# A long transform split 64 by 32 instead of 32 by 64, with its short stages as 64-row and 64-column TensorE tiles

## Chip, cores, metric

One core of one Trainium2 chip. The metric is the device time of one execution in microseconds (us), the median of several. A run over 1.5% above the fastest of its kernel is called slow, the others fast; only fast ones are compared here. The median of the kernel before lies between 343.3 and 345.9 us over the rounds, so kernels are compared through their ratio to the kernel before, which ran in the same rounds on the same chip.

## The reference, cut to what matters

```python
def reference(...):
    x = A_u                                             # 1 x 2048 x 640
    g = sigmoid((x * gate_w).sum(-1, keepdims=True))
    a = A(x, ...)     # K[d, l] = Re sum_n C exp(dt A l) dt B ; a = causal convolution of u with K
                      # along l (written with rfft / irfft of length 4096) + u * Dskip
    b = (gelu(x @ w_gate) * (x @ w_up)) @ w_down        # 640 -> 1728 -> 640
    return g * a + (1 - g) * b
```

The kernel does the feed-forward half as ordinary matmuls. The convolution half generates samples of K ("contraction", on TensorE), transforms K and u in two stages A and B, multiplies the spectra ("chain"), and transforms back in two stages (the second one is "finish"). Between two stages the data have to change partitions, and they do that by being written to DRAM (tensors dU, dKA, dY) and read back in another order. The channels are treated in two halves of W = 320.

## The kernel before: what the change and the argument touch

The order of instructions is made by a small list scheduler in the kernel itself (class `Plan`), which knows estimated costs and a table `P` of ranks. It counts every transfer as 0.45 us of SP's time and a fixed time per KB. All working tiles are slices of one large SBUF tile called `arena`.

```python
def contract(h):                                        # samples of K: 640 matmuls of 32 columns for each half
    for b in range(nb):
        for i in range(16):
            for q in range(2):
                for cg in range(4):
                    c = 16 * (b0 + b) + i
                    nc.tensor.matmul(ps[32 * cg:32 * cg + NE, k + b, 32 * i:32 * i + 32],
                                     lhsT=cs2[:, q, c, cg:4 * NE:4], rhs=cs1[:, q, c, cg:128:4],
                                     start=(q == 0), stop=(q == 1))
    ...
    src = kst[32 * cg + e0:32 * cg + e0 + n, :, :]      # stores of the samples to dS, 20 for each half

def stageB(src, key, dst, name, c, R):                  # src is dU[h] or dKA[h], a DRAM tensor [32, 128, W]
    v = src[:].rearrange("i (l k) w -> (i l) k w", l=4)
    dma(640, lambda: nc.sync.dma_start(out=bi[s][:], in_=v[:, 8 * c:8 * c + 8, :]), r=key, w=[f"bi{s}"], rank=R)
    for a in range(4):
        def go(k, a=a):
            for b in range(2):
                nc.tensor.matmul(ps[:, k + b, 0:W], lhsT=TB[:, 0, :], rhs=bi[s][:, 2 * a + b, :], start=True, stop=True)
        ...

def chain(h, R):
    ...
            for b in range(2):
                for m, x in ((1, U[c]), (2, Us[c])):    # Us is U with real and imaginary rows swapped, by two transfers
                    nc.tensor.matmul(ps[:, k + b, 0:W], lhsT=TB[:, m, :], rhs=x[:, 2 * a + b, :], start=(m == 1), stop=(m == 2))
    ...
    dma(640, lambda c=c, t=t: nc.sync.dma_start(
        out=dY[h][:].rearrange("i (l k) w -> (i l) k w", l=4)[:, 8 * c:8 * c + 8, :], in_=t[:]), ...)
```

## Time and profile before

| | before |
|---|---|
| time, median of 3 (all) | 343.45 us (342.25, 343.45, 344.82) |
| busy PE, DVE, ACT | 79%, 69%, 64% of the profiled 344.3 us |
| contraction 1, first to last piece | 101.4 to 117.7 us |
| contraction 2 | 183.1 to 201.9 us |
| last phase, after contraction 2 | 142 us |

First lines of the profile's page of the kernel before. The rows under "busy tenths" cut the span in 40 slices; a 9 means busy for 90% or more; the DMA row is the mean busy share of 16 DMA engines. PE stands for TensorE's matmuls and PEld for its weight loads, DVE for VectorE, ACT for ScalarE, POOL for GpSimd; SP is SyncE, which issues the transfers (SPq is its queue). L678 is line 678 of the kernel; `ps` is PSUM, where the matmuls write.

```profile
span 344.3 us, 6849 instructions
## 1 busy us (share of the span) xinstructions
PE 273.3 (79%) x2785; PEld 155.4 (45%) x2798; DVE 238.2 (69%) x331; ACT 220.5 (64%) x302; POOL 4.0 (1%) x15
...
PE   0289999988994699999995267439699999899953
...
DMA  7972222455543223453256529757999799996495
GB/s 242 343 247 57 77 78 76 134 171 151 155 116 101 66 34 76 131 182 83 76 146 136 105 38 216 167 166 176 307 344 351 243 295 305 256 345 204 165 321 163
```

Three phases are to be seen: a start of some 100 us in which ACT and DVE generate the samples' factors; a middle; and from about the 28th slice a last phase in which the DMA engines are nearly full. Windows of 20 us from that last phase (length; busy us and number of instructions of PE, PEld, DVE, ACT and POOL in turn; granted TensorE clock as a share of full speed; DMA share; GB/s):

```profile
300.00:320.00 20.00, 19.50 (x138) 13.19 (x137) 18.60 (x26) 9.02 (x14) 0.00 (x0) 1.00 0.81 257
280.00:300.00 20.00, 17.34 (x122) 11.60 (x121) 12.44 (x15) 10.03 (x16) 0.00 (x0) 1.00 1.04 290
```

The chain of waits (the work that ended last, followed back) names, in the last phase, transfers of 640 KB between 3 and 14 us long (start, length, what):

```profile
275.14 7.86 DMA arena<-dU
282.99 9.39 DMA arena<-dKA
292.39 14.44 DMA arena<-dY
...
321.94 2.92 DMA dY<-arena
```

The second contraction on PE (start, length, line, count, and in brackets the idle time before). PE is idle for 2 to 5 us between pieces although nothing that the profile shows holds it ("issue"):

```profile
183.08 1.52 PE L678 MATMUL ps<-arena 128*20 128x32 bf16 x161
186.74 1.24 PE L678 MATMUL ps<-arena 128*20 128x32 bf16 x128 [2.14 <-issue]
193.21 1.24 PE L678 MATMUL ps<-arena 128*20 128x32 bf16 x128 [5.23 <-issue]
196.94 1.25 PE L678 MATMUL ps<-arena 128*20 128x32 bf16 x128 [2.48 <-issue]
```

### The profile page before, as it was taken

The page shows a single profiled execution, that of the slowest core. Times are in us where ns is not written, and L with a number is a line of the kernel's source. Part 1 is how long each engine was busy: PE and PEld are TensorE (multiplying, and loading weights), DVE is VectorE, ACT ScalarE, POOL GpSimd, SP SyncE. Part 2 cuts the span into 40 slices and gives each one's busy share as a digit, 9 for nine tenths or more (in the row PEclk, how much of TensorE's full clock was granted, in tenths as well). Part 3 has the DMA queues.
Part 4 walks back from the last instruction along what each step waited for, and adds up shares of the span by engine and source line. Part 5 has one row for each costly group of instructions (what it writes and reads, how often), then busy time and mean ns, then how long its engine had stood idle before and what let it go on. Part 6 is the DMA issues. An engine that isn't in the chain of part 4 may idle for free.

```text
span 344.3 us, 6849 instructions
## 1 busy us (share of the span) xinstructions
PE 273.3 (79%) x2785; PEld 155.4 (45%) x2798; DVE 238.2 (69%) x331; ACT 220.5 (64%) x302; POOL 4.0 (1%) x15
## 2 busy tenths in 40 slices
PE   0289999988994699999995267439699999899953
PEld 0044444433673367544443243214346666566731
DVE  5969887999894258698973044524649865799364
ACT  4999986996894499788995046534547853525200
POOL 3000000000000000000000000000000000000000
PEclk9999999999998589999998569858989999999995
DMA  7972222455543223453256529757999799996495
GB/s 242 343 247 57 77 78 76 134 171 151 155 116 101 66 34 76 131 182 83 76 146 136 105 38 216 167 166 176 307 344 351 243 295 305 256 345 204 165 321 163
DMA packets 57989, 60.66 MB, mean 176 GB/s; under 512 B 9475, under 2 KB 53318, under 8 KB 57926
## 3 DMA queue, kind: packets, MB, share of 16 engines
q1 hardware_dynamic: 57958, 60.23, 61.1%
q8 instruction: 22, 0.36, 0.4%
q14 instruction: 9, 0.07, 0.1%
HBM read 35.80 MB, written 19.17 MB: 160 GB/s over the span
## 4 chain that ended last, share of the span: by engine, by line
PE 49%; DMA 25%; SPq 9%; issue 8%; DVE 4%; ACT 2%; DVEq 0%; ACTq 0%
PE ps L530 16%; PE ps L578 12%; PE ps L550 10%; DMA arena<-dY 8%; PE ps L880 4%; SPq L707 3%; PE ps L678 3%; DMA arena<-dKA 3%; ACT arena L289 2%; DMA arena<-in_params_dram 2%; DMA arena<-in_w_gu_dram 2%; DMA arena<-dU 2%; PE ps L748 2%; DMA arena<-in_u_nat_dram 2%; DMA dKA<-arena 2%
## 5 line engine op out<-in xcount | busy, mean ns | idle before, releaser
L289 ACT CAST arena<-ps 128x640 bf16<-128x640 f32 (+2 forms) x110 | 69.4, 692 | 65.8 <-DVE arena L293 26.1
L530 PE MATMUL ps<-arena 128*128 128x512 bf16 x274 | 65.0, 388 | 16.9 <-DMA arena<-in_w_gu_dram 16.0
L550 PE MATMUL ps<-arena 128*128 128x512 bf16 x253 | 63.1, 397 | 13.8 <-DMA arena<-in_w_gu_dram 10.3
L293 DVE CAST arena<-ps 128x640 bf16<-128x640 f32 (+2 forms) x62 | 48.4, 800 | 36.6 <-PE ps L678 21.7
L578 PE MATMUL ps<-arena 128*128 128x320 bf16 x448 | 65.2, 306 | 0.5 <-ACT arena L289 0.3
L578 PEld LDWEIGHTS <-arena 128*128 128x128 bf16 x448 | 44.6, 100 | 19.6 <-issue 1.3
L530 PEld LDWEIGHTS <-arena 128*128 128x128 bf16 x280 | 27.6, 99 | 50.6 <-DMA arena<-in_w_gu_dram 16.0
L550 PEld LDWEIGHTS <-arena 128*128 128x128 bf16 x260 | 26.2, 101 | 46.9 <-DMA arena<-in_w_gu_dram 11.7
L554 DVE TENSOR_TENSOR arena<-ps,arena 128x1024 bf16<-128x1024 f32 x26 | 31.7, 1219 | 18.6 <-PE ps L550 16.2
L618 ACT ACTIVATE arena<-arena 128x2560 bf16<-128x2560 int16 x18 | 41.6, 2340 | 1.6 <-DVE arena L614 1.5
L534 ACT ACTIVATE arena<-ps 128x1024 bf16<-128x1024 f32 (+1 forms) x28 | 27.1, 1024 | 7.6 <-PE ps L530 7.4
L678 PE MATMUL ps<-arena 128*20 128x32 bf16 x1280 | 12.7, 198 | 18.6 <-issue 18.6
L851 PE MATMUL ps<-arena 128*128 128x320 bf16 x128 | 22.6, 310 | 5.6 <-DMA arena<-dU 3.0
L639 DVE TENSOR_TENSOR arena<-arena 128x2560 bf16<-128x2560 bf16 x16 | 23.0, 1484 | 3.8 <-ACT arena L618 3.8
L628 ACT ACTIVATE arena<-arena 128x320 bf16<-128x320 f32 x64 | 23.2, 454 | 0.9 <-DVE arena L481 0.9
L678 PEld LDWEIGHTS <-arena 128*20 128x20 bf16 x1280 | 11.3, 99 | 20.3 <-issue 20.3
L295 DVE TENSOR_SCALAR arena<-ps,omg 128x640 bf16<-128x640 f32 x9 | 7.9, 882 | 18.0 <-PE ps L578 17.9
L851 PEld LDWEIGHTS <-arena 128*128 128x128 bf16 x128 | 12.5, 101 | 14.7 <-DMA arena<-dU 3.8
L880 PE MATMUL ps<-arena 128*128 128x320 bf16 x128 | 18.7, 299 | 0.0
L904 DVE SCALAR_TENSOR_TENSOR arena<-ps,g_f,arena 128x320 bf16<-128x320 f32 x32 | 15.4, 544 | 2.7 <-PE ps L898 2.7
L666 DVE TENSOR_TENSOR arena<-arena 128x2560 bf16<-128x2560 bf16 x10 | 14.9, 1486 | 3.2 <-ACT arena L618 3.1
L612 DVE SCALAR_TENSOR_TENSOR arena<-arena 128x320 int32<-128x320 f32 x40 | 16.9, 483 | 0.0
(89 smaller groups left out, 225.2 us busy)
## 6 DMA issues: line engine op xcount, KB each, us to landing
arena<-in_w_gu_dram SPq DMA_DIRECT2D x52, 160.0 KB
dU<-arena SPq DMA_DIRECT2D x32, 160.0 KB
arena<-dU SPq DMA_DIRECT2D x8, 640.0 KB
arena<-arena SPq DMA_DIRECT2D x16, 320.0 KB
dKA<-arena SPq DMA_DIRECT2D x8, 640.0 KB
arena<-dKA SPq DMA_DIRECT2D x8, 640.0 KB
dY<-arena SPq DMA_DIRECT2D x8, 640.0 KB
arena<-dY SPq DMA_DIRECT2D x8, 640.0 KB
```

The costliest lines, as they stand in the source:

```text
L289: nc.scalar.copy(out=dst, in_=src(b))
L293: nc.vector.tensor_copy(out=dst, in_=src(b))
L530: nc.tensor.matmul(ps[:, k + j, :], lhsT=Wg[w][:, kt, :], rhs=xT[2 * grp + j][:, kt, :], start=(kt == 0), stop=(kt == NKT - 1))
L534: add({"ACT": an(1024)}, lambda s: nc.scalar.activation(out=HTall[0:p, :, f, :], in_=ps[0:p, plan.bank(g):plan.bank(g) + 2, :], func=ACT.G ...
L550: nc.tensor.matmul(ps[:, k + j, :], lhsT=Wu[w][:, kt, :], rhs=xT[2 * grp + j][:, kt, :], start=(kt == 0), stop=(kt == NKT - 1))
L554: add({"DVE": v1(1024)}, lambda s: nc.vector.tensor_tensor(out=HTall[:, :, f, :], in0=ps[:, plan.bank(u):plan.bank(u) + 2, :], in1=HTall[: ...
L578: nc.tensor.matmul(ps[:, k + h, 0:W], lhsT=HTq[q][:, f, 128 * j:128 * j + 128], rhs=Wd[f][:, W * h:W * h + W], start=(f == 0), stop=(f == ...
L618: ac(an(2 * n * W), lambda: nc.scalar.activation(out=t[:], in_=ph.bitcast(I16)[:, :, :, 0:32:2], func=ACT.Sin, scale=SIN_SCALE), r=[f"ph{k ...
L628: nc.scalar.activation(out=cs1[:, 1, :, 4 * s:4 * s + 4], in_=quads(aT[:, ds]), func=ACT.Exp, scale=float(sg * (4 + 8 * i)))
L678: nc.tensor.matmul(ps[32 * cg:32 * cg + NE, k + b, 32 * i:32 * i + 32], lhsT=cs2[:, q, c, cg:4 * NE:4], rhs=cs1[:, q, c, cg:128:4], start= ...
L851: nc.tensor.matmul(ps[:, k + b, 0:W], lhsT=TB[:, 0, :], rhs=bi[s][:, 2 * a + b, :], start=True, stop=True)
L880: nc.tensor.matmul(ps[:, k + b, 0:W], lhsT=TB[:, m, :], rhs=x[:, 2 * a + b, :], start=(m == 1), stop=(m == 2))
```

## The change

The intent: less TensorE work. With a split of 64 by 32 the second, the inverse and the last stage have only 64 rows to sum over, or 64 columns to produce, and four (or two) such matmuls are put on separate quarters (or halves) of the array. The contraction takes four channels ("quads") together in one matmul of 80 columns, and only one quarter of the result is used; its samples then lie on every fourth partition. A third weight buffer, earlier loads and a new table of ranks come with it.

The diff, cut to its core (cuts are marked):

```diff
-    P = dict(sw=5.4, gate=1.91, up=2.5, gelu=8.59, ...)
+    P = dict(sw=40.82, gate=13.77, up=4.13, gelu=8.47, ...)          # 25 values became 38
...
-    Wg = [at(O_W + 1280 * k, [128, NKT, 128], BF16, f"Wg{k}") for k in range(2)]
+    Wg = [at(O_W + 1280 * k, [128, NKT, 128], BF16, f"Wg{k}") for k in range(3)]
...
-    kst = at(O_TAIL + 2560, [128, 32, 80], BF16, "kst")
+    kst = at(O_KST, [128, 80, 80], BF16, "kst")
...
-    dY = [dp.tile([32, 128, W], BF16, name=f"dY{h}") for h in range(2)]
+    dY = [dp.tile([64, 64, W], BF16, name=f"dY{h}") for h in range(2)]
...
     def contract(h):
+            for i in range(n):
+                for q in range(2):
+                    nc.tensor.matmul(ps[:, k + i // g, 80 * (i % g):80 * (i % g) + 80], lhsT=cs1[:, q, k0 + i, :],
+                                     rhs=cs2[:, q, k0 + i, :], start=(q == 0), stop=(q == 1))
...
-                    src = kst[32 * cg + e0:32 * cg + e0 + n, :, :]
+                    src = kv[c:128:4, e0:e0 + n, c, :]               # kv is kst with its columns seen as (e j)
...
     def stageB(src, key, dst, name, c, R):
-        v = src[:].rearrange("i (l k) w -> (i l) k w", l=4)
-        dma(640, lambda: nc.sync.dma_start(out=bi[s][:], in_=v[:, 8 * c:8 * c + 8, :]), r=key, w=[f"bi{s}"], rank=R)
+        v = src[:].rearrange("i (l k s) w -> k (i l) s w", l=2, k=2)
+        dma(640, lambda: nc.sync.dma_start(out=bi[s][:], in_=v[:, :, 8 * c:8 * c + 8, :]), r=key, w=[f"bi{s}"], rank=R)
...
                 for b in range(2):
-                    nc.tensor.matmul(ps[:, k + b, 0:W], lhsT=TB[:, 0, :], rhs=bi[s][:, 2 * a + b, :], start=True, stop=True)
+                    for x in range(2):
+                        nc.tensor.matmul(ps[64 * b:64 * b + 64, k + x, 0:W], lhsT=TB[64 * x:64 * x + 64, 0, :],
+                                         rhs=bi[s][64 * x:64 * x + 64, 2 * a + b, :], start=True, stop=True)
...
-                dma(320, lambda c=c, s=s: nc.sync.dma_start(out=Us[c][64 * s:64 * s + 64], in_=U[c][64 - 64 * s:128 - 64 * s]),
+                dma(320, lambda c=c, s=s: nc.sync.dma_start(out=Us[c][s:128:2], in_=U[c][1 - s:128:2]),
...
-                out=dY[h][:].rearrange("i (l k) w -> (i l) k w", l=4)[:, 8 * c:8 * c + 8, :], in_=t[:]),
+                out=dY[h][:].rearrange("i (k s) w -> k i s w", k=2)[:, :, 8 * c:8 * c + 8, :], in_=t[:]),
...                                                                    (chain and finish: tiles likewise)
```

## The prediction, made before any run of the changed kernel

> **What bounds the kernel now.** No single engine: the page shows PE 79% of 344.3 us, DVE 69%, ACT 64%. The table of 10-us windows shows three phases.
> (1) 0-105 us, to the first kernel contraction (L678): ACT busy 92.7 of the first 110 us, DVE nearly as full; PE starts dense work only at 25 us: the chain of waits runs through parameter and weight loads until then.
> (2) Contractions at 105-118 and 183-202 us, 640 matmuls of 128x32 each. PE is fed too slowly: the chain shows "issue" gaps of 1.2 to 5.2 us between their pieces, and the granted clock falls to 0.50 (windows 110:120, 190:200), so that the next 28 matmuls of L578 take 6.16 us instead of 3.80.
> (3) 202-344 us: transposes through DRAM. DMA share is 0.94 to 1.10 in most windows of 240-310, PE 85-98% busy; the chain alternates DMA (dU, dKA, dY) with PE.
>
> **What the change does.**
> - Contraction: 1280 small matmuls become 320 of 128x80 with K=128 (three quarters of it waste). The logits (80 weight loads with one-column matmuls in 2.1 us) show 26 ns a pair as a floor; 80 columns add at most 33 ns (320 take 136 ns in L880). Estimate 50-60 ns each: 8-10 us a contraction instead of 13 and 19, without the slow clock. Cost: copies out of PSUM grow from 2560 to 6400 columns[...], shared by ACT and DVE.
> - Stages B, chain, finish: L851, L880, L898 are 320 matmuls of about 136 ns, 43 us. [...]
> - DMA: same bytes and run lengths, eight more issues. No gain.
> - Third weight buffer, earlier x and weight loads, new ranks: PE can start near 10 us instead of 25; the 26 us of waits on in_w_gu (L530, L550) mostly go.
> - ACT table loads: 27 against 22 by the order of instructions, 1.28 us each: +6 us.
>
> **On the critical path.** By the new order, ACT has about 83 us of work before it copies contraction 1 (before: about 95), so it lies near 92-98 us, 10 us earlier. From there to contraction 2 ACT has about 83 us (before 67, with 12 idle): unloading moved into this stretch. So contraction 2 starts at 180-188, hardly earlier, but ends at 188-197 instead of 202. Front gain: 8-10 us. Phase 3 holds about 120 us of DMA work (window shares summed from 200 us), so it can't shrink by all of PE's 15-20 us; I take 10-14 us of its 142. Together -18 to -24.
>
> **Prediction: 321 us, 8 in 10 between 307 and 336.** Faster by over 2%: 0.87; within 2%: 0.10; slower: 0.03.
>
> **What would show each step.** L684 under 10 us per contraction, granted clock above 0.5 after it; PE dense from 10 us; contraction 2 over before 197; matmuls of L834 spaced 34-45 ns; PE busy below 250 us; ACT 220-230; the last phase 125-135 us long, DMA share near 1 and a DMA-heavy chain.
>
> **What would make it wrong.** Tiles that don't overlap, or weight loads that block them (phase 3 gains nothing, 330+); copies out of PSUM slower than 1.2 us per 960 columns; contractions bound by ACT rather than PE; or phase 3 bound by PE and latency rather than DMA throughput, in which case more comes (below 307).

The "15-20 us" of PE that the last phase names were the author's estimate of what the tiles save of the 43 us, and the trace of before gave no number for it, so the 10-14 us rest on something not shown (measured later: 10.5 us of PE, e3). The longer copies out of PSUM: added up, their durations in the traces are 14.0 us for both contractions after against 6.7 before, 3.6 us more for each. For 80 columns, a quarter of the 136 ns of L880 is 34; 960 columns took 0.96 us on ACT and 1.16 us on DVE in the changed kernel.

## The result, and the profile after

The changed kernel takes **593.08 us** (592.62 to 593.79, 4 runs) against 343.94 us for the kernel before in the same rounds: a ratio of 1.7256, with a 95% interval from 1.7183 to 1.7329. The result is correct. Ratios here are the mean time of one kernel's fast runs over that of the other's fast runs of the same rounds, so they are not quite the ratio of the medians quoted.

The page of the changed kernel:

```profile
span 591.0 us, 5498 instructions
## 1 busy us (share of the span) xinstructions
PE 287.3 (49%) x2082; PEld 157.2 (27%) x2094; DVE 241.1 (41%) x337; ACT 227.1 (38%) x306; POOL 4.9 (1%) x15
...
PE   3587999259999706346360160244020604246033
...
DMA  8722123114455217324332321121211211342258
GB/s 272 246 56 68 55 77 87 24 38 116 126 157 164 71 55 194 117 77 132 113 112 93 111 96 63 53 92 54 92 53 53 89 52 53 127 128 93 70 135 238
```

The busy times of the engines hardly changed, so the added 249 us are waiting. And the DMA row, which was full in the last phase before, is at 1 and 2 there: the DMA engines are not overloaded, they are *unused*. Two windows of the last phase:

```profile
300.00:320.00 20.00, 5.78 (x38) 2.47 (x36) 7.99 (x10) 8.30 (x10) 0.00 (x0) 0.63 0.13 53
440.00:460.00 20.00, 0.00 (x0) 0.00 (x0) 1.67 (x3) 0.00 (x0) 0.00 (x0) 0.55 0.13 53
```

The last two columns are the key. A share of 0.13 of 16 engines is 2.1 engines, and they move 53 GB/s, that is 26 GB/s for each of two. The slices of the page show the same 52 to 54 GB/s again and again. The chain shows what it is that waits:

```profile
296.55 12.44 DMA arena<-dKA
308.99 31.10 DMA dKA<-arena
...
365.03 30.39 DMA dY<-arena
...
420.25 40.19 DMA arena<-dU
...
484.21 41.79 DMA dY<-arena
```

Transfers of 640 KB that took 3 to 14 us in the chain of before take 12 to 42 us here, queueing included; only the loads from dY stay at 5 to 6. `dKA<-arena` is in this list although its code did not change.

The contraction, on TensorE, did what was hoped. The second one of the changed kernel:

```profile
198.88 3.60 PE L684 MATMUL ps<-arena 128*128 128x80 bf16 x96
230.61 2.46 PE L684 MATMUL ps<-arena 128*128 128x80 bf16 x64
```

160 matmuls in 6.1 us of PE time instead of 640 in pieces spread over 19 us (the gap between the two pieces here is a wait for a transfer), and no "issue" gap. What went are these gaps, 18.6 us over both contractions of the kernel before; PE's busy time on them is the same (12.7 us before, 12.3 after, for both together). The matmuls start 36 ns apart (median).

### The profile page after: what moved, and what is told of

The parts are those of the page before. It is cut to its first block, busy times and chain, and to the rows that moved or that the text cites. A ratio compares the mean times of both kernels' runs of the same rounds, so it can differ in the third digit from the quotient of the medians.

```text
span 591.0 us, 5498 instructions
## 1 busy us (share of the span) xinstructions
PE 287.3 (49%) x2082; PEld 157.2 (27%) x2094; DVE 241.1 (41%) x337; ACT 227.1 (38%) x306; POOL 4.9 (1%) x15
## 4 chain that ended last, share of the span: by engine, by line
DMA 48%; PE 21%; ACT 11%; SPq 10%; DVE 8%; issue 2%; DVEq 0%; ACTq 0%
DMA dY<-arena 17%; DMA arena<-dU 9%; PE ps L580 6%; DMA arena<-dKA 6%; DMA dKA<-arena 5%; PE ps L532 5%; PE ps L552 5%; SPq L845 4%; DMA arena<-dS 4%; ACT arena L291 3%; SPq L829 3%; DMA dS<-arena 2%; ACT arena L630 2%; DMA arena<-dY 2%; DVE arena L556 2%
## 5 line engine op out<-in xcount | busy, mean ns | idle before, releaser
L291 ACT CAST arena<-ps 128x640 bf16<-128x640 f32 (+1 forms) x112 | 73.6, 719 | 238.5 <-PE ps L834 166.4
L295 DVE CAST arena<-ps 128x640 bf16<-128x640 f32 (+1 forms) x62 | 50.5, 841 | 214.0 <-PE ps L834 127.1
L834 PE MATMUL ps<-arena 64*64 64x320 bf16 x256 | 22.2, 422 | 165.6 <-DMA arena<-dKA 81.3
L580 PE MATMUL ps<-arena 128*128 128x320 bf16 x448 | 77.0, 339 | 23.8 <-ACT arena L291 16.3
L532 PE MATMUL ps<-arena 128*128 128x512 bf16 x274 | 68.4, 405 | 19.6 <-DMA arena<-in_u_T_dram 9.1
L552 PE MATMUL ps<-arena 128*128 128x512 bf16 x254 | 61.3, 396 | 2.2 <-DMA arena<-in_w_gu_dram 1.1
L834 PEld LDWEIGHTS <-arena 64*64 64x64 bf16 x256 | 10.0, 138 | 177.7 <-DMA arena<-dKA 83.5
L818 PE MATMUL ps<-arena 128*128 128x320 bf16 x64 | 14.2, 361 | 39.6 <-DMA arena<-dS 24.3
L630 ACT ACTIVATE arena<-arena 128x320 bf16<-128x320 f32 x64 | 23.4, 454 | 6.8 <-DMA dS<-arena 5.9
L885 PE MATMUL ps<-arena 128*64 128x320 bf16 x64 | 8.5, 400 | 31.4 <-DMA arena<-dY 31.3
L658 ACT ACTIVATE arena<-arena 128x320 bf16<-128x320 f32 x40 | 15.0, 456 | 19.8 <-DMA dS<-arena 19.6
L818 PEld LDWEIGHTS <-arena 128*128 128x128 bf16 x64 | 7.1, 113 | 45.9 <-issue 41.9
L661 DVE TENSOR_TENSOR arena<-arena 128x1280 bf16<-128x1280 bf16 x10 | 8.0, 820 | 25.5 <-DMA dS<-arena 17.8
L751 PE MATMUL ps<-arena 128*128 128x320 bf16 x64 | 12.5, 319 | 10.4 <-DMA arena<-in_u_nat_dram 7.2
```

The source lines that it names most:

```text
L291: nc.scalar.copy(out=dst, in_=src(b))
L295: nc.vector.tensor_copy(out=dst, in_=src(b))
L532: nc.tensor.matmul(ps[:, k + j, :], lhsT=Wg[w][:, kt, :], rhs=xT[2 * grp + j][:, kt, :], start=(kt == 0), stop=(kt == NKT - 1))
L552: nc.tensor.matmul(ps[:, k + j, :], lhsT=Wu[w][:, kt, :], rhs=xT[2 * grp + j][:, kt, :], start=(kt == 0), stop=(kt == NKT - 1))
L580: nc.tensor.matmul(ps[:, k + h, 0:W], lhsT=HTq[q][:, f, 128 * j:128 * j + 128], rhs=Wd[f][:, W * h:W * h + W], start=(f == 0), stop=(f == ...
L630: nc.scalar.activation(out=cs1[:, 1, :, 4 * s:4 * s + 4], in_=quads(aT[:, ds]), func=ACT.Exp, scale=float(sg * (4 + 8 * i)))
```

## Experiments

**Theory S** (spread): the 16 loads of stage B and the 8 stores to dY have an access pattern whose outermost dimension has size 2 (`k`), and therefore each runs on 2 of the 16 DMA engines. The trace agrees with two engines (0.13 of 16, at 53 GB/s, in the windows 300:320 and 440:460). The pattern of before, `(i l) k w`, has 128 outermost, and the DMA share there reaches 1.04 (280:300, 290 GB/s). That the outermost dimension is the cause is at this point a conjecture from these two patterns; e1 and e4 test it.
**Rival F**: the change also introduced transfers that step over partitions (`c:128:4`, `s:128:2`), and the trace shows waits that the data do not call for; such false waits string everything up.
**Rival P**: the tiles or the new order themselves are bad.

A transfer of 640 KB at 53 GB/s takes 655,360 B / 53 GB/s = 12.4 us, as the first line of the chain above does; 24 of them are 297 us one after another.

### e1: every such transfer issued as two, of 64 rows each

```diff
-        dma(640, lambda: nc.sync.dma_start(out=bi[s][:], in_=v[:, :, 8 * c:8 * c + 8, :]), r=key, ...)
+        def load():
+            for x in range(2):
+                nc.sync.dma_start(out=bi[s][64 * x:64 * x + 64], in_=v[x, :, 8 * c:8 * c + 8, :])
+        dma(640, load, r=key, ...)
...                                     (the stores to dY likewise)
```

> The changed kernel, but each of the 24 transfers whose access pattern has an outermost dimension of 2 (16 loads of the second stage, 8 stores to dY) is issued as two transfers of 64 rows; nothing else, the engines' order is the same. Theory S (an outermost dimension of 2 puts a transfer on 2 of the 16 DMA engines: 53 GB/s and DMA share 0.13 in the windows 300:320 and 440:460): time falls from 593 to 345-380 us, and no window shows a long stretch at 53 GB/s. Rival F (false waits for transfers with a partition step dominate): stays over 500. Rival P (TensorE tiles or the new order): stays near 590.

Measured: correct, **362.06 us** (360.94 to 363.47), ratio 1.0486 to before (1.0412 to 1.056). One edit of the access patterns takes away 231 of the 249 us. Its page, in the rows that answer to those above:

```profile
DMA  6973230222231025255658687338999998896996
GB/s 218 323 236 94 80 85 19 58 84 80 60 88 29 6 61 154 76 157 140 180 147 205 126 234 198 147 92 188 252 238 306 301 284 263 253 327 191 286 307 176
```

The 9s are back in the last phase, and no slice of it stands at 53 GB/s. A store to dY in its chain:

```profile
286.53 7.37 DMA dY<-arena
```

In its windows 260:280 and 280:300 the DMA share is 1.06 and 1.03, at 270 and 311 GB/s. P is refuted as the main cause: tiles and order are unchanged here.

### e2: without the transfers that step over partitions, spread left as it was

The samples get an SBUF tile of their own instead of a slice of `arena`; the spectrum gets its real and imaginary rows in blocks of 32 partitions, so that the swapping copies move whole blocks.

```diff
+    arenak = mp.tile([128, (K1 - K0) // 2], BF16, name="arenak")     # holds kst and the two trig buffers
...
-    FIELDS = ((0, 1), (2, 15), (1, 1), (1, 31), (0, 1), (0, 63), (6, 1))
+    FIELDS = ((0, 1), (2, 15), (1, 1), (0, 31), (5, 1), (0, 63), (6, 1))
-                    out=Us[c][s:128:2], in_=U[c][1 - s:128:2]),
+                    for b in (32 * s, 64 + 32 * s):
+                        nc.sync.dma_start(out=Us[c][b:b + 32], in_=U[c][b ^ 32:(b ^ 32) + 32])
```

> The changed kernel with its 2-engine transfers left in, but without transfers that step over partitions: the kernel samples lie in a tile of their own, and the spectrum has real rows and imaginary rows in blocks of 32, so that the swapped copy moves whole blocks. Theory S: removes only the waits of ACT for dS between 98 and 131 us, about 25-30 us, and something after 200 us: 540-575 us. Rival F: falls below 420. Rival P: stays near 590.

Measured: correct, **574.52 us** (2 runs), ratio 1.6617. 18.6 us less than the changed kernel: at the upper end of the range for S (I had expected 25 to 30 us from these waits), and far from what F expects. F is a second, small cause.

### e3: both

> Both edits. Theory S with F as a second cause: 310-335 us, faster than before (344), about what was predicted blind. If P is right: over 400.

Measured: correct, **343.39 us** (341.93 to 344.31), ratio 0.9928 (0.9867 to 0.9989). The expectation (310-335) is missed: with both faults gone the change is worth less than 1%, not the 22 us of the prediction.

### e4: the fault put into the kernel before

```diff
-        v = src[:].rearrange("i (l k) w -> (i l) k w", l=4)
+        v = src[:].rearrange("i (l k) w -> (i l) k w", l=4).rearrange("(q t) k w -> t q k w", t=2)
...                                     (the store to dY likewise)
```

> The kernel before, with the outermost dimension 2 put into the same 24 transfers (rows 2q+t go to partition 64t+q, so the result is wrong on purpose; same bytes, same runs of 5120 bytes, same instructions on every engine). Theory S: 24 transfers of 655 KB at 53 GB/s are 12.4 us each, 297 us on two engines, against about 125 us of the last phase: 500-600 us. Rivals F and P: unchanged, 340-350.

Measured: **582.88 us** (2 runs), ratio 1.6859, wrong result. The bytes, the runs, every instruction of every engine and their order are those of before; only the order of the dimensions differs. Its page has 52 to 54 GB/s in eight slices of its second half, as the changed kernel has again and again. Together with e1 this shows S in both directions.

### e5: which of the false waits counts

As e3, but the swapping copies keep their step of 2 partitions; only the samples have their own tile.

> The changed kernel with the transfers split (e1) and the kernel samples in a tile of their own, but the swapped spectrum still copied with a partition step of 2. Of the 19 us between e1 (362) and e3 (343), the trace of e1 shows ACT idle for about 25 us in 100-140 us behind the stores of the samples. If the samples are the whole of the false waits: 341-347 us. If the swapped copies, also with a partition step, matter too: 348-358.

Measured: correct, **342.96 us** (340.87 to 343.85), ratio 0.9908: the samples are the whole of it. The waits of e1 that disappear (who waits, for whom: us in total, times, longest):

```profile
ACT arena L658 <- DMA dS<-arena: 19.3, 4, 6.6
DVE arena L661 <- DMA dS<-arena: 17.8, 3, 9.5
DVE arena L661 <- ACT arena L630: 7.3, 1, 7.3
ACT arena L630 <- DMA dS<-arena: 5.9, 1, 5.9
```

```profile
SPq L710 <- ACT arena L658: 12.6, 5, 4.3
SPq L710 <- DVE arena L661: 7.9, 4, 2.2
```

L710 issues the stores of the samples (reading `kst`), L658 and L661 write the factors for the second half (`cs2`). They share no byte, yet they wait for each other in turn. In e5 the same lines (here L667 and L670) are idle for 0.0 and 2.1 us (the two numbers at the end of the first part of each line are busy us and mean ns; then comes idle time):

```profile
L667 ACT ACTIVATE arena<-arena 128x320 bf16<-128x320 f32 x40 | 14.6, 454 | 0.0
...
L670 DVE TENSOR_TENSOR arena<-arena 128x1280 bf16<-128x1280 bf16 x10 | 7.9, 818 | 2.1 <-ACT arena L667 2.1
```

That the waits vanish with a separate tile is shown. That they came from the framework, which places the semaphores and may have taken a store with a step of four partitions to touch other parts of the same tile, is argued. For it speaks that the same lines of the kernel before (L653, L656) are idle for 0.0 us; its waits for stores of samples, 9.2 and 8.7 us before L786 and L788, are real ones, since these lines write a tile (`WAT`) that overlaps `kst`. Against it speaks that the swapping copies, with their step of 2, cost nothing in e5. The change also moved `kst` next to `cs2` and gave its stores a step in the columns; no run separates these from the step of four.

### e6: only the loads split, the stores to dY left on two engines

> The changed kernel with only the 16 loads of the second stage split; the 8 stores to dY stay on an outermost dimension of 2. Theory S, if stalls add up by bytes on two engines: stores are a third of the 297 us, so 8 x 12.3 = 98 us stay serial: 410-450 us. If the stores hardly matter: 362-375.

Measured: correct, **434.25 us** (2 runs), ratio 1.2557. The 8 stores cost 434 - 362 = 72 us (of the 98 us if nothing overlapped), the 16 loads the other 159 us. Both count, roughly by their bytes.

### e7: is the tiles' saving on the critical path?

```diff
-                for b in range(2):
+                for b in (0, 1, 0, 1):                               # stage B; chain and finish likewise
```

> e3 with every matmul of the second, inverse and last stages issued twice (the same result): PE in the last phase has back what the tiles saved, about 20-24 us of PE. If the tiles' saving lies on the critical path: 343 + 12 to 22 = 355-365 us. If it lies off it, hidden under transfers and waits for them: 343-350 us.

Measured: correct, **346.04 us** (345.99 to 346.63), ratio 1.0011 (0.9959 to 1.0063). Against e3's ratio of 0.9928 that is 0.8%, 3 us (0 to 6 by the two intervals, an estimate). Doubling the 576 matmuls adds 15.9 us of busy time on their three lines (57.7 against 41.9 in e3), less than the 20-24 expected, but more than the 10.5 us that the tiles had saved there (52.4 in the kernel before); about 3 us of it reach the end. This also gives the cleanest reading of the tiles, because here PE has enough in a row (start, length, count):

```profile
265.86 2.37 PE L881 MATMUL ps<-arena 64*64 64x320 bf16 x64
```

64 in 2.37 us, 37 ns each; in the kernel before the same stage takes 5.33 us for 38, 140 ns each:

```profile
264.87 5.33 PE L880 MATMUL ps<-arena 128*128 128x320 bf16 x38
```

The change doubles the number of matmuls of stage B and the chain (256 for 128), so at this rate their PE time would fall to one half. By the starts in the trace eight successive ones take 272 ns against 1,087 before, the full factor of four for each. Every one of them has its own weight load, of 109 ns on average for 64x64 in e7 (L881) against 98 for a full one in the kernel before (L880); in this unbroken stretch that costs nothing.

### e8: is the contraction's length on the critical path?

```diff
-                    for q in range(2):
+                    for q in (0, 1, 0, 1):
```

> e3 with every matmul of the two contractions issued twice (the same result): 160 more of 40 to 50 ns in each. If the contractions are on the critical path with their full length: 343 + 12 to 17 = 355-360 us. If only one of them: +6 to 8, 349-352. If none: 343-346.

Measured: correct, **350.24 us**; the three fast runs are 348.00, 349.42 and 351.05, ratio 1.0106 (1.0037 to 1.0174). Against e3 that is 1.8%, 6 us, for 320 x 36 ns = 11.5 us of added PE (an estimate from e3's spacing; the expectation took 40 to 50 ns for each): about one of the two contractions' worth. The remaining run, the profiled one, took 1,479 us and is left out: PE's matmuls of 512 columns started 1,278 ns apart in it instead of 216, with a recorded clock of 1.00. I have no explanation; no other run showed it.

### e9: is the last phase bound by the bytes it moves?

```diff
-                    out=Us[c][s:128:2], in_=U[c][1 - s:128:2]),
+                    out=Us[c][s:128:2, 0:1, :], in_=U[c][1 - s:128:2, 0:1, :]),
```

> e5 with the 16 copies of the swapped spectrum cut to an eighth of their bytes (one of eight rows; wrong on purpose), with the same issues, waits and order: 4.6 MB less of about 36 MB that the last phase moves. If the last phase is bound by the throughput of the DMA engines: at 300 GB/s 15 us less, 328-333 us against 343. If it is bound by the order and latency of single transfers and waits: 338-343.

Measured: **334.40 us** (333.47 to 336.11), wrong result, ratio 0.9789 (0.9728 to 0.985). Against e5 that is 8.6 us by the medians and 4 us by the ratios (the fast runs of the kernel before were themselves about 4 us faster in these rounds, so the ratios count; 1 to 7 us by the two intervals, an estimate). It lies between the two expectations: throughput matters, for about a quarter of the 15 us expected if nothing else did. The 300 GB/s of the expectation are a round estimate: the windows of before show 257 and 290.

### e10: the same work in another order

In e5, the issue costs seen in the traces (0.6 us for a store of samples or a swap, 1.2 us for a transfer issued as two) are put into the kernel's scheduler, and a random search looks for ranks that make its own estimate shortest.

> e5 with the issue costs that the traces show put into the kernel's own scheduler (0.6 us for each issue of a sample store and of a swap, 1.2 us for a transfer issued as two, instead of 0.45) and its ranks searched anew. The work is the same, the order alone differs. If the gain was lost to an order tuned for other costs: 330-338 us. If the order is near what the transfers allow: 339-345.

Measured: correct, **335.15 us** (333.50 to 336.37, 6 runs), ratio **0.9788** (0.9742 to 0.9835). A version that is faster than the kernel before by 2.1% (whether by more than 2% the interval leaves unclear). Against e5, whose work is the same, it is 1.2%, 4 us, by the ratios. What moved is contraction 2:

```profile
173.15 3.60 PE L690 MATMUL ps<-arena 128*128 128x80 bf16 x96
180.87 2.45 PE L690 MATMUL ps<-arena 128*128 128x80 bf16 x64
```

In e3 its two pieces stood at 180.13 and 193.51, with 16 matmuls of stage A between them that waited 5.5 us for gathers from DRAM; the same 16 stand between them here and wait 1.3 us. The contraction ends 13 us earlier, of which 4 reach the end.

### e11: the stores of samples issued by POOL

> As e10, with the 40 stores of kernel samples issued by POOL instead of SP, and ranks searched for that. If SP's queue, where 20 sample stores of 0.6 us stand before the second half's gathers, holds up the last phase: 325-335 us. If not: 339-348, and the stores may take longer there.

Measured: correct, **334.05 us** (332.81 to 335.04), ratio 0.976 (0.9707 to 0.9814). It lies in the range set for "SP's queue holds up the last phase", but e10 without this edit had already come to its edge, so the range cannot tell the two apart. The same as e10 within the intervals: SP's queue is not what holds the last phase, or an order that relieves it loses as much elsewhere.

### e12: the kernel before, ranked anew in the same way

> The kernel before, with the measured issue costs (0.75 us for a store of samples, 0.6 us for a swap) in its scheduler and its ranks searched anew in the same way as e10. If e10's gain over the kernel before comes from the new order alone and the change's work is worth nothing: 333-338 us, like e10. If the changed stages are worth their 8 us themselves: 341-346, like before. In between, both share it.

In the trace of before a store of samples keeps SP for a median of 0.64 us (mean 0.69), a swap for 0.60; the 0.75 is what was put into the scheduler.

Measured: correct, **363.79 us** (361.17 to 365.23, 6 runs), ratio 1.0546. A miss: no reading of mine allowed for it. The search found an order that the scheduler's own estimate preferred, and the chip runs it 5% slower; the profile shows waits of 17.6 us (DVE) and 15.6 us (PE) behind weight loads, and contraction 2 stretched from 186 to 208 us by "issue" gaps of more than 4 us. So an order alone moved the repaired kernel by -1.2% (e10 against e5) and the kernel before by +5.5%. How much of e10's 2.1% is the change's work and how much a lucky order stays open.

## Why the prediction was wrong, point by point

The prediction of 321 us missed by 272 us. The terms, from the runs:

| term | predicted | measured |
|---|---|---|
| transfers with outermost dimension 2 | 0 ("No gain") | +231 us (e1 against after) |
| false waits around the stores of samples | not seen | +19 us (e5 against e1) |
| everything else the change does | -22 us | -2.5 us (e3, ratio 0.9928) |

1. **The step that failed** is, in its words, "DMA: same bytes and run lengths, eight more issues. No gain." Bytes and run lengths are indeed the same, and that is not what decides. `-> k (i l) s w` in place of `-> (i l) k w` put a dimension of 2 outermost, and each of 24 transfers ran on two engines (53 GB/s at a DMA share of 0.13 in the windows 300:320 and 440:460; e1 and e4). The clue stood in the diff; I compared sizes and did not look at the order of dimensions. The worst case that I listed (330 us and over) was still about TensorE.
2. An ordinary transfer suffers too: `dKA<-arena`, unchanged, stands in the chain with 31.1 us. The trace shows the time; that it queues behind the slow ones on those two engines is argued from it. Issuing got slow too: a store to dY kept SP for a median of 0.32 us before and 1.58 us (up to 12.1) in the changed kernel.
3. **False waits** were in reach as well: the order of instructions with their waits shows ACT's writes waiting for transfers. I compared the order and not the waits.
4. **Front: right in kind.** Contraction 1 starts at 91.0 us in e3 (predicted 92-98) and contraction 2 ends at 196.2 (predicted 188-197). Only the gain was smaller: 5.7 us against before's 201.9, not 8-10. It still holds in the changed kernel up to the point where its transfers begin: contraction 1 at 90.4. PE started at 9.7 us in e3, as predicted, but was not dense after it: 5.58 and 4.42 us busy in the windows 20:30 and 50:60. ACT was busy for 9.94 us in each of them.
5. **Spacing of the matmuls: right in kind.** 36 ns a matmul of the contraction (predicted 50-60), 34 ns for a tile matmul in e7's unbroken stretch (predicted 34-45); granted clock around contraction 1 1.00 in e3 (90:110) against 0.50 before (110:120); ACT busy 227.1 us in the changed kernel (predicted 220-230). **Too large: the saving.** The prediction took 15-20 us from the three tile stages and PE busy below 250 us. In e3 these stages are busy for 41.9 us instead of 52.4, 10.5 us less, and PE for 267.6 us instead of 273.3. The inverse stage (in `chain`) in before and in e3, whose 256 matmuls come in 11 shorter pieces, with a median of 422 ns for eight successive ones; why they are slower than in e7 is not shown:

```profile
L880 PE MATMUL ps<-arena 128*128 128x320 bf16 x128 | 18.7, 299 | 0.0
L881 PE MATMUL ps<-arena 64*64 64x320 bf16 x256 | 13.8, 343 | 1.6 <-ACT arena L299 0.7 <-ACT arena L301 0.3
```

**Wrong in worth:** I credited the last phase with 10-14 us; e7 shows that about 3 us of the 15.9 put back lie on the critical path. The windows of the last phase in e3, then in before:

```profile
196.00:343.00 147.00, 106.28 (x953) 57.99 (x949) 84.91 (x103) 59.20 (x89) 1.41 (x1) 0.86 0.88 234
```

```profile
202.00:345.00 143.00, 112.65 (x685) 67.86 (x686) 90.55 (x111) 63.34 (x92) 0.00 (x0) 0.91 0.84 244
```

PE has 6 us less to do and the phase is 4 us longer, at a DMA share of 0.88 against 0.84. This phase, 84% full of transfers before the change, did not shrink although PE had time, and e9 shows that taking bytes away does shorten it. The remaining difference between 343 and 321 (last phase +4 us instead of -10 to -14, front 3 us short) is thus located but not explained: the 24 added issues of the repair, the order, and transfers may all have a share. The order alone was worth 4 us in e10 and cost the kernel before 18 us in e12.

## What to carry to other kernels

When a change rewrites an access pattern of a transfer, look at its outermost dimension (here on the DRAM side) and not only at bytes and run lengths: a 2 there left all but two of the 16 DMA engines idle for long stretches, and the sign of it was a DMA share of 0.13, near 2/16, with the compute engines waiting for transfers. Issuing the transfer once for each value of that dimension was the remedy here (593 to 362 us). And before crediting saved PE time, ask what fills the same stretch: here putting back more than the tiles had saved cost about 3 us.
